# Score products of two attention units in a row in a banded attention and token/channel mixing kernel

## The chip, the cores and the metric

The kernel runs on one core of a Trainium2 chip. The metric is the device time of one execution in microseconds (us); several executions of each kernel are timed, and the median is compared. One more execution is profiled, and all rows of traces below come from it.

## What is computed

A banded softmax attention (batch 2, 8 heads, 768 positions, head size 64) feeds two mixing layers.

```python
# attention: keys kept are the first 8 (n_global) and the last 96 (n_local) up to the query's own
scores = q @ k.T / sqrt(64) - slope[h] * dist        # where kept, else -1e9
a = exp(scores - max(scores)); a = a / (sum(a) + 1e-9)
x = (a @ v) as [2, 768, 512]                          # heads side by side
# token and channel mixing
u = x + (relu(x.T @ w_tok1) @ w_tok2).T
x = u + relu(u @ w_ch1) @ w_ch2
# rotation, second token mixing, last channel layer
theta = x @ w_theta; zr = x * cos(theta); zi = x * sin(theta)
u = x + w_tok_r @ zr + w_tok_i @ zi
out = u + relu(u @ w_ch)
```

The weights arrive as 64-bit words, and the kernel itself turns them into pairs of a high and a low part. A product of mixing layers is three matmuls on such pairs (high by high, high by low, low by high).

## The kernel before

All layers run one after another; the change touches the first, the banded attention, which takes the first 105 us or so. Each engine runs its own instructions strictly in the order in which the program writes them down (a manual schedule), and instructions of different engines wait for each other through semaphores that are put in automatically: a tile that is to be written again waits for the last reader of what was in it, even where that reader stands further down in the program.

**Units.** The attention is cut into 24 units. Unit u covers one batch, one pair of heads (j = 0, 1) and two blocks of 128 queries (ii = 0, 1). Three units make a pair of heads (ip = 0, 1, 2), so there are eight pairs of heads, and each has its own q, k and v from memory. In the first unit of a pair (ip = 0) the first query block sees 128 keys and not 256.

**Stages of a unit.**

- Scores (L434): four products of 64 rows by 256 columns (128 where ip = 0 and ii = 0), two for each head. A head occupies 64 of the 128 rows of TensorE, so the products of the two heads lie in different halves of it. Each product is traced as two matmuls. They write two PSUM tiles `s` (tag `s`, 4 buffers).
- VectorE adds the bias and finds the minimum (L447, four instructions for a unit), ScalarE takes exponentials (four), both in the tiles `e0`, `e1`.
- Turn (L481): up to eight transpositions of 128x128 into two PSUM tiles `t` (2 buffers), copied out to `at0` and `at1`, one copy each, by ScalarE (L493), or, for j = 0 and in passes that start a weight job, by VectorE (L491).
- Values (L403): up to eight products with v, each traced as two matmuls, into the PSUM tile `o` (one buffer). Odd units below 12 write tile `m` instead (one buffer). Then `finish_rows` on VectorE (L387, L391, L396) divides by the sums and frees the PSUM tile, and GpSimd splits the result (L376, L379).

**Passes.** The loop over u makes pass u out of the scores of unit u, the turn of unit u-1 and the values of unit u-2, the transpositions and value products alternating. The last two exponentials of unit u are issued within the turn (`between`). From pass 14 on each pass ends with `fill`: two (later one) parts of the token mixing of the batch that is already through, six matmuls of 512 columns in all (L93, out `mm`), and at the very end the transpositions `columns` (L760, out `ut`).

**Loads.** In a pass with ip = 1 the program writes, after the values, on GpSimd the two memsets of the next pair's v tiles (L357), and on the one DMA queue (SP), in this order: v of the next pair (L364, L366, L367), then q and k of the pair after it (L335, L336). The tiles of v, q and k have two buffers each. The raw weight loads (L122) go through the same queue.

**Weight jobs.** One 128x512 piece of weights is converted in four phases, one phase in each pass: scale (ScalarE, L136 and L137), join (VectorE L142 and L145, then GpSimd L146), high (ScalarE L154), low (VectorE L157). `STARTS` says in which passes a job starts. In a pass without a start the VectorE phases stand right behind the four L447; in a pass with a start they stand within the turn. Seven jobs are for the token mixing; `EARLY` more are pieces of the first channel blocks, of which every block has two. The other channel pieces are converted in the same four phases later: a phase is advanced at every `tick`, three ticks during the token mixing that follows, and then one after every half of `up` (L93, out `gp`) for batch 0. A piece must be through before `up` or `down` of its block reads it.

Of the kernel before, what the change touches and what calls it, by code (L numbers as in the profile page):

```python
# [15 lines left out]
F32 = mybir.dt.float32  # L16
# [9 lines left out]
P = 128  # L26
# [22 lines left out]
WARM_FILL = (4, 2)  # L49
# [12 lines left out]
def r(ap):  # L62
    return ap.bitcast(F32R)
# [17 lines left out]
class Build:  # L81
# [326 lines left out]
    def attention_band(self, pairs_pool, first, h1):  # L408
# [5 lines left out]
        ps_, half = self.ps, len(units) // 2  # L414
        with tc.tile_pool(name="au", bufs=2) as up, tc.tile_pool(name="aa", bufs=2) as ap:

            def scores(u):
                b, hp, ip = units[u]
                t = pairs[(b, hp)]
                n = "_%d" % u  # L420
                mn = up.tile([P, 2, 2], F32, name="mn" + n, tag="mn", bufs=4)
                es = []
                for j in range(2):
                    es.append(up.tile([P, 2, 2 * P], F32, name="e%d" % j + n, tag="e%d" % j))
                ps = [
                    ps_.tile([P, 2, 2 * P], F32, name="s%d" % j + n, tag="s") for j in range(2)
                ]
                kf = t["k"].rearrange("p n w -> p (n w)")
                for ii in range(2):
                    i = 2 * ip + ii  # L430
                    c0 = P if i == 0 else 0
                    for j in range(2):
                        pj = slice(j * D, (j + 1) * D)
                        nc.tensor.matmul(  # L434
                            ps[j][:, ii, c0:],
                            lhsT=t["q"][pj, i * P : (i + 1) * P],
                            rhs=kf[pj, i * KW - P + c0 : i * KW + P],
                            start=True,
                            stop=True,
                        )  # L440
                exps = []
                for ii in range(2):
                    i = 2 * ip + ii
                    c0 = P if i == 0 else 0
                    for j in range(2):
                        e = es[j][:, ii, c0:]
                        nc.vector.tensor_tensor_reduce(  # L447
                            out=e,
                            in0=ps[j][:, ii, c0:],
                            in1=self.base[2 * hp + j][min(i, 1)],  # L450
                            op0=ALU.add,
                            op1=ALU.min,
                            scale=-SCALE,
                            scalar=BIGNUM,
                            accum_out=mn[:, ii, j : j + 1],
                        )
                        exps.append(functools.partial(
                            nc.scalar.activation,
                            out=e,
                            in_=e,  # L460
                            func=AF.Exp,
                            bias=mn[:, ii, j : j + 1],
                            scale=-1.0,
                        ))
                st[u] = dict(e=es)
                return exps

            def turn(u, dve, between):


                b, hp, ip = units[u]
                n = "_%d" % u
                e = st[u]["e"]
                st[u]["at"] = at = []

                def one(j, ii, c):
                    if len(at) == j:
                        at.append(ap.tile([P, 2, 2, P], F32, name="at%d" % j + n, tag="at%d" % j))
                        st[u]["pt"] = ps_.tile([P, 2, 2, P], F32, name="t%d" % j + n, tag="t")
                    pt = st[u]["pt"]  # L480
                    nc.tensor.transpose(  # L481
                        pt[:, ii, c, :], e[j][:, ii, c * P : (c + 1) * P], self.ident
                    )
                    if ii == c == 1:
                        c0 = 1 if ip == 0 else 0
                        pf = pt.rearrange("p a c w -> p (a c) w")[:, c0:, :]
                        af = at[j].rearrange("p a c w -> p (a c) w")[:, c0:, :]
                        if j == 1:
                            between()
                        if j == 0 and dve:  # L490
                            nc.vector.tensor_copy(out=af, in_=pf)  # L491
                        else:
                            nc.scalar.copy(out=af, in_=pf)  # L493

                return [
                    functools.partial(one, j, ii, c)
                    for j in range(2)
                    for ii in range(2)
                    for c in range(2)
                    if ip or ii or c  # L500
                ]
# [32 lines left out]
            N = len(units)  # L534
            fill = collections.defaultdict(list)

            def mix1(b, tb, s, tag):
                return functools.partial(self.token_part, tag, h1, b, tb, s)

            def mix2(s):  # L540
                return functools.partial(self.token_row, "m", h1, 0, s)

            def columns(s):
                return functools.partial(self.turn_row, "t", 0, s)

            for n in range(2 * NS):
                tb, s = divmod(n, NS)
                fill[half + 2 + n // 2].append(mix1(0, tb, s, "m"))
            for s in range(NS):
                fill[N - 4 + s].append(mix2(s))  # L550
            for s in range(4):
                fill[N - 2 + s].append(columns(s))
            for tb in range(NT):
                for s in range(NS - 2):
                    fill[N + 1].append(mix1(1, tb, s, "s"))
            self.load_v(first, 0, 0)
            self.token_jobs()
            pairs[order[1]] = self.load_qk(pairs_pool, *order[1], bufs=2)
            for u in range(N + 2):
                start = u in self.STARTS  # L560
                on_dve, on_act = self.split_tick(start)
                exps = []
                if u < N:
                    b, hp, ip = units[u]
                    oi = u // (NS // 2)
                    exps = scores(u)
                    if u < len(WARM_FILL):
                        self.warm_up(WARM_FILL[u])
                if not start:
                    on_dve()  # L570
                for step in exps[:2]:
                    step()

                def between(late=exps[2:]):
                    for step in late:
                        step()
                    if start:
                        on_dve()
                    on_act()

                turned = 0 <= u - 1 < N
                if not turned:
                    between()
                self.run_steps(
                    turn(u - 1, start and u < N - 4, between) if turned else [],
                    values(u - 2) if 0 <= u - 2 < N else [],
                )
                for step in fill.pop(u, ()):
                    step()
                if u < N and oi + 1 < len(order) and ip == 1:  # L590
                    nx = order[oi + 1]
                    self.tiles_v(pairs_pool, pairs[nx], *nx)
                    self.load_v(pairs[nx], *nx)
                    if oi == 0:
                        self.prefetch(1)
                    if oi + 2 < len(order):
                        pairs[order[oi + 2]] = self.load_qk(pairs_pool, *order[oi + 2], bufs=2)
# [165 lines left out]
    def token_jobs(self):  # L763
# [15 lines left out]

        for i in range(self.EARLY):  # L780
            self.channel_job(*divmod(i, 2))
# [31 lines left out]
    def run(self):  # L813
        nc, tc, dram = self.nc, self.tc, self.dram
        with ExitStack() as es:
# [23 lines left out]

            we = es.enter_context(tc.tile_pool(name="we", bufs=self.EARLY, side="right"))  # L840
            self.early = we
            self.wc = [[None, None] for _ in range(NF)]
            for i in range(self.EARLY):
                self.channel_piece(we, *divmod(i, 2))
# [29 lines left out]
                self.moe(es, a8s, w12p, h1)  # L874

    KW12 = 9
    EARLY = 4
    STARTS = (5, 8, 11, 13, 14, 16, 17, 18, 20, 21, 22)

    def moe_jobs(self, ws, w12p):  # L880

# [6 lines left out]
        for i in range(2 * NF):  # L888
            self.wc_job[divmod(i, 2)] = 0 if i < self.EARLY else self.channel_job(*divmod(i, 2))

# [126 lines left out]
class PhaseB:  # L1017
# [23 lines left out]
    def turn(self, i):  # L1041
        b, s = self.todo[i]
        t = self.xt[i] = self.xtbuf(i)
        x = self.k.x[b][:, s, :]
        self.k.turn_rows("t", x, r(t[:, 0]), r(t[:, 1]), "xt_%d_%dp" % (b, s))
# [239 lines left out]
```

## Time and profile before

| | |
|---|---|
| median of 3 runs | 506.6 us (506.12 to 506.81) |
| the profiled execution, its own time | 506.85 us |
| its span, from the first to the last instruction | 505.1 us |
| TensorE matmul busy | 499.5 us, 99% |
| VectorE, ScalarE, GpSimd busy | 61%, 47%, 32% |

The span is what the trace covers; 1.75 us of the profiled execution's time lie around it. Ends of matmuls are modelled, so rows of TensorE are read by their starts: the distance from one start to the next is what an instruction costs.

### The profile page before, as it was taken

How to read it: one execution, taken by the hardware profiler on the slowest of the kernel's cores; microseconds unless marked ns; L12 is line 12 of the kernel's file. 1: busy time of each engine (PE TensorE's matmuls, PEld its weight loads, DVE VectorE, ACT ScalarE, POOL GpSimd, SP SyncE). 2: the span in 40 equal slices, each digit the busy share in tenths (PEclk: the TensorE clock that was granted, in tenths of full speed). 3: DMA queues.
4: the chain of work that ended last, by engine and by line, in shares of the span. 5: the costliest groups of instructions: out<-in, count | busy, mean ns of one | idle time of the engine just before them, and what ended most of it. 6: DMA issues, size and time to landing. Idle time of an engine off the chain costs nothing.

```text
span 505.1 us, 7724 instructions
## 1 busy us (share of the span) xinstructions
PE 499.5 (99%) x2908; PEld 421.1 (83%) x2908; DVE 309.3 (61%) x671; ACT 235.7 (47%) x458; POOL 163.4 (32%) x175
## 2 busy tenths in 40 slices
PE   9999999999999999999999999999999999999997
PEld 4888878887888888888888888888888889888886
DVE  4688878736877575216473565377888876351342
ACT  6798778714755554113554544435555343222010
POOL 7355444410343333001332151154555533223000
PEclk9999999999999999999999999999999999999999
DMA  6697764202453443002333121222210000000012
GB/s 192 201 262 242 233 212 141 84 3 65 148 150 124 135 126 94 0 1 76 120 120 102 42 78 48 84 84 84 80 46 1 1 1 0 22 21 22 21 64 103
DMA packets 30013, 45.93 MB, mean 91 GB/s; under 512 B 1936, under 2 KB 20880, under 8 KB 29968
## 3 DMA queue, kind: packets, MB, share of 16 engines
q1 hardware_dynamic: 29968, 45.36, 28.8%
q8 instruction: 25, 0.41, 0.3%
q14 instruction: 20, 0.16, 0.1%
HBM read 42.21 MB, written 3.15 MB: 90 GB/s over the span
## 4 chain that ended last, share of the span: by engine, by line
PE 95%; SPq 1%; DMA 1%; ACT 1%; DVE 1%; issue 0%; ACTq 0%
PE gp L93 20%; PE y L93 20%; PE h L93 19%; PE th L93 7%; PE v L93 7%; PE mm L93 6%; PE o L403 6%; PE t L481 4%; PE s L434 4%; DMA k<-k 1%; PE ut L760 1%; SPq L856 0%; DVE xl L710 0%; ACT xh L704 0%; PE xt_1p L760 0%
## 5 line engine op out<-in xcount | busy, mean ns | idle before, releaser
L146 POOL TENSOR_TENSOR cvt<-cvt,cvs 128x512 int32<-128x512 int32 (+1 forms) x57 | 75.8, 1330 | 219.8 <-DVE cvt L145 175.3
L93 PE MATMUL h<-wc,g 128*128 128x512 f32 x432 | 102.1, 390 | 0.0
L93 PE MATMUL gp<-xh,wc 128*128 128x512 f32 (+1 forms) x384 | 99.1, 339 | 0.1
L93 PEld LDWEIGHTS h<-wc,g 128*128 128x128 f32 x432 | 79.6, 188 | 15.4
L706 DVE SCALAR_TENSOR_TENSOR g<-gp,g 128x512 fp32r<-128x512 f32 (+1 forms) x48 | 26.7, 557 | 85.7 <-ACT g L704 85.7
L93 PEld LDWEIGHTS gp<-xh,wc 128*128 128x128 f32 x384 | 67.1, 188 | 9.7 <-DVE xl L710 0.3
L93 PE MATMUL gp<-xl,wc 128*128 128x512 f32 (+1 forms) x192 | 64.9, 338 | 0.0
L704 ACT ACTIVATE g<-gp 128x512 fp32r<-128x512 f32 (+1 forms) x48 | 23.4, 488 | 72.5 <-PE gp L93 72.5
L93 PE MATMUL y<-wri,z 128*128 128x256 f32 (+1 forms) x288 | 52.9, 338 | 0.0
L93 PE MATMUL y<-wri,s 128*128 128x256 f32 (+1 forms) x288 | 52.8, 338 | 0.0
L93 PEld LDWEIGHTS y<-wri,s 128*128 128x128 f32 x288 | 44.8, 188 | 6.8
L93 PEld LDWEIGHTS y<-wri,z 128*128 128x128 f32 x288 | 44.8, 188 | 6.8
L481 PE MATMUL t<-ident,e 128*128 128x128 f32 x176 | 48.1, 285 | 0.3 <-ACT at L493 0.3
L142 DVE SCALAR_TENSOR_TENSOR cvs<-cvt,cvs 128x512 int32<-128x512 int32 (+1 forms) x57 | 44.4, 778 | 0.0
L93 PEld LDWEIGHTS gp<-xl,wc 128*128 128x128 f32 x192 | 36.1, 188 | 5.1
L481 PEld LDWEIGHTS t<-ident,e 128*128 128x128 f32 x176 | 31.7, 184 | 8.1 <-ACT at L493 2.2
L447 DVE CUSTOM_DVE_ANT_0 e<-s,base 128x256 f32<-128x256 f32 (+1 forms) x96 | 32.8, 398 | 9.2 <-PE s L434 8.5
L136 ACT ACTIVATE cvt<-raw 128x512 f32<-128x512 f32 (+1 forms) x57 | 37.3, 655 | 1.9 <-issue 1.9
L137 ACT ACTIVATE cvs<-raw 128x512 int32<-128x512 uint16 (+1 forms) x57 | 37.3, 654 | 0.0
L1075 ACT ACTIVATE w<-w 128x512 f32<-128x512 f32 x12 | 7.6, 633 | 57.3 <-DVE w L1072 57.3
L403 PE MATMUL o<-v,at 128*128 128x65 f32 x192 | 32.3, 252 | 0.0
L403 PEld LDWEIGHTS o<-v,at 128*128 128x128 f32 x192 | 29.8, 196 | 0.0
(136 smaller groups left out, 814.0 us busy)
## 6 DMA issues: line engine op xcount, KB each, us to landing
raw<-w_ch SPq DMA_DIRECT2D x28, 512.0 KB, 3.6
raw<-w_tok SPq DMA_DIRECT2D x21, 512.0 KB, 3.5
k<-k SPq DMA_DIRECT2D x7, 480.0 KB, 5.7
v<-v SPq DMA_DIRECT2D x8, 384.0 KB, 3.7
out<-o SPq DMA_DIRECT2D x11, 256.0 KB, 2.0
q<-q SPq DMA_DIRECT2D x7, 384.0 KB, 5.0
raw<-w_theta SPq DMA_DIRECT2D x4, 512.0 KB, 3.6
a<-v SPq DMA_DIRECT2D x8, 240.0 KB, 4.5
```

What stands on the lines that cost most here:

```text
L93: self.nc.tensor.matmul(out, lhsT=a, rhs=b, start=first and i == 0, stop=last and i == n - 1)
L136: nc.scalar.activation(out=f(t), in_=f(top), func=AF.Copy, scale=2.0**-111)
L137: nc.scalar.activation(out=s, in_=nxt, func=AF.Copy, scale=2.0**-13)
L142: nc.vector.scalar_tensor_tensor(out=s, in0=t, scalar=-(1 << 31), in1=s, op0=ALU.bitwise_and, op1=ALU.bitwise_or)
L146: nc.gpsimd.tensor_tensor(out=t, in0=t, in1=s, op=ALU.add)
L403: self.nc.tensor.matmul(po[:, j * OW : j * OW + D + 1], lhsT=at, rhs=v[:, j * (D + 1) : (j + 1) * (D + 1)], start=first, stop=last,)
L434: nc.tensor.matmul(ps[j][:, ii, c0:], lhsT=t["q"][pj, i * P : (i + 1) * P], rhs=kf[pj, i * KW - P + c0 : i * KW + P], start=True, stop=True,)
L447: nc.vector.tensor_tensor_reduce(out=e, in0=ps[j][:, ii, c0:], in1=self.base[2 * hp + j][min(i, 1)], op0=ALU.add, op1=ALU.min, scale=-SCAL ...
L481: nc.tensor.transpose(pt[:, ii, c, :], e[j][:, ii, c * P : (c + 1) * P], self.ident)
L704: nc.scalar.activation(out=hi, in_=ps, func=AF.Relu if relu else AF.Copy)
L706: nc.vector.scalar_tensor_tensor(out=lo, in0=ps, scalar=0.0, in1=f(hi), op0=ALU.max, op1=ALU.subtract)
L1075: nc.scalar.activation(out=a, in_=t, func=AF.Abs)
```

## The change

The score products of two units are issued one behind the other: units 0 and 1 (with the warm-up matmuls between them), unit 2 alone, then 3 and 4, 5 and 6, and so on to 21 and 22, and 23 alone, each pair in the odd pass. The turn and the values move one pass back (turn of u-2 and values of u-3 in pass u), so the loop has one pass more and `fill` moves by one. The exponentials wait in a list `late`, from which four are issued at the start of an odd pass and two at each of two places later on. The tiles `e0` and `e1` get four buffers instead of two. `EARLY` goes from 4 to 2, so two pieces (channel block 1) are no longer converted during the attention but first in the mixing, and `STARTS` has 9 passes instead of 11.

```diff
--- before.py
+++ after.py
@@ -421,7 +421,9 @@
                 mn = up.tile([P, 2, 2], F32, name="mn" + n, tag="mn", bufs=4)
                 es = []
                 for j in range(2):
-                    es.append(up.tile([P, 2, 2 * P], F32, name="e%d" % j + n, tag="e%d" % j))
+                    es.append(
+                        up.tile([P, 2, 2 * P], F32, name="e%d" % j + n, tag="e%d" % j, bufs=4)
+                    )
                 ps = [
                     ps_.tile([P, 2, 2 * P], F32, name="s%d" % j + n, tag="s") for j in range(2)
                 ]
@@ -465,7 +467,7 @@
                 st[u] = dict(e=es)
                 return exps
 
-            def turn(u, dve, between):
+            def turn(u, dve, first, second):
 
 
                 b, hp, ip = units[u]
@@ -485,8 +487,7 @@
                         c0 = 1 if ip == 0 else 0
                         pf = pt.rearrange("p a c w -> p (a c) w")[:, c0:, :]
                         af = at[j].rearrange("p a c w -> p (a c) w")[:, c0:, :]
-                        if j == 1:
-                            between()
+                        (first, second)[j]()
                         if j == 0 and dve:
                             nc.vector.tensor_copy(out=af, in_=pf)
                         else:
@@ -545,45 +546,59 @@
 
             for n in range(2 * NS):
                 tb, s = divmod(n, NS)
-                fill[half + 2 + n // 2].append(mix1(0, tb, s, "m"))
+                fill[half + 3 + n // 2].append(mix1(0, tb, s, "m"))
             for s in range(NS):
-                fill[N - 4 + s].append(mix2(s))
+                fill[N - 3 + s].append(mix2(s))
             for s in range(4):
-                fill[N - 2 + s].append(columns(s))
+                fill[N - 1 + s].append(columns(s))
             for tb in range(NT):
                 for s in range(NS - 2):
-                    fill[N + 1].append(mix1(1, tb, s, "s"))
+                    fill[N + 2].append(mix1(1, tb, s, "s"))
             self.load_v(first, 0, 0)
             self.token_jobs()
             pairs[order[1]] = self.load_qk(pairs_pool, *order[1], bufs=2)
-            for u in range(N + 2):
+
+
+            late = []
+
+            def emit(n):
+                for _ in range(min(n, len(late))):
+                    late.pop(0)()
+
+            for u in range(N + 3):
                 start = u in self.STARTS
                 on_dve, on_act = self.split_tick(start)
-                exps = []
+                new = {0: (0, 1), 1: (), 2: (2,)}.get(u, (u, u + 1) if u % 2 else ())
+                for n in new:
+                    if n < N:
+                        late += scores(n)
+                        if n < len(WARM_FILL):
+                            self.warm_up(WARM_FILL[n])
+                if new:
+                    emit(4)
                 if u < N:
                     b, hp, ip = units[u]
                     oi = u // (NS // 2)
-                    exps = scores(u)
-                    if u < len(WARM_FILL):
-                        self.warm_up(WARM_FILL[u])
                 if not start:
                     on_dve()
-                for step in exps[:2]:
-                    step()
-
-                def between(late=exps[2:]):
-                    for step in late:
-                        step()
+
+                def first():
+                    if not new:
+                        emit(2)
+
+                def second():
+                    emit(2)
                     if start:
                         on_dve()
                     on_act()
 
-                turned = 0 <= u - 1 < N
+                turned = 0 <= u - 2 < N
                 if not turned:
-                    between()
+                    first()
+                    second()
                 self.run_steps(
-                    turn(u - 1, start and u < N - 4, between) if turned else [],
-                    values(u - 2) if 0 <= u - 2 < N else [],
+                    turn(u - 2, start and u < N - 3, first, second) if turned else [],
+                    values(u - 3) if 0 <= u - 3 < N else [],
                 )
                 for step in fill.pop(u, ()):
                     step()
@@ -874,8 +889,8 @@
                 self.moe(es, a8s, w12p, h1)
 
     KW12 = 9
-    EARLY = 4
-    STARTS = (5, 8, 11, 13, 14, 16, 17, 18, 20, 21, 22)
+    EARLY = 2
+    STARTS = (6, 9, 12, 14, 15, 17, 18, 20, 22)
 
     def moe_jobs(self, ws, w12p):
```

## Rows read from the trace of the kernel before

**Rows 1.** The page, busy time of the engines, share of the span, instructions.

```profile
PE 499.5 (99%) x2908; PEld 421.1 (83%) x2908; DVE 309.3 (61%) x671; ACT 235.7 (47%) x458; POOL 163.4 (32%) x175
```

**Rows 2.** Timeline of TensorE around unit 7: start, length, line, instructions merged.

```profile
26.80 0.34 PE L403 MATMUL o<-v,at 128*128 128x65 f32 x2
...
28.13 0.33 PE L481 MATMUL t<-ident,e 128*128 128x128 f32 x1
28.29 0.33 PE L403 MATMUL o<-a,at 128*128 128x65 f32 x2
28.46 0.28 PE L481 MATMUL t<-ident,e 128*128 128x128 f32 x1
28.58 0.34 PE L403 MATMUL o<-v,at 128*128 128x65 f32 x2
```

**Rows 3.** The same unit's score matmuls, from three narrow windows of that timeline.

```profile
27.07 0.70 PE L434 MATMUL s<-k,q 64*128 64x256 f32 x3
...
27.39 0.59 PE L434 MATMUL s<-k,q 64*128 64x256 f32 x3
...
27.81 0.38 PE L434 MATMUL s<-k,q 64*128 64x256 f32 x2
```

**Rows 4.** Timeline of TensorE, scores of units 3, 4, 6 and two first transpositions.

```profile
11.36 0.33 PE L481 MATMUL t<-ident,e 128*128 128x128 f32 x1
...
13.95 0.93 PE L434 MATMUL s<-k,q 64*128 64x128 f32 x8 [0.44 <-DMA k<-k]
14.81 0.33 PE L481 MATMUL t<-ident,e 128*128 128x128 f32 x1
...
17.24 1.14 PE L434 MATMUL s<-k,q 64*128 64x256 f32 x8
...
23.77 0.93 PE L434 MATMUL s<-k,q 64*128 64x128 f32 x8
```

**Rows 5.** Timeline of the DMA queue: keys of the third pair, v of the fifth, keys of the sixth.

```profile
15.82 1.62 SPq L336 DMA_DIRECT2D k<-k  x1
...
42.57 0.38 SPq L364 DMA_DIRECT2D v<-v  x1
...
45.17 0.42 SPq L336 DMA_DIRECT2D k<-k  x1
```

**Rows 6.** Tile k, windows around the issues at 15.82 and at 45.17.

```profile
DMA to landing us min/median/max: 7.1/7.1/7.1
...
DMA to landing us min/median/max: 5.5/5.5/5.5
```

**Rows 7.** The page, costliest groups: the reduction of the scores.

```profile
L447 DVE CUSTOM_DVE_ANT_0 e<-s,base 128x256 f32<-128x256 f32 (+1 forms) x96 | 32.8, 398 | 9.2 <-PE s L434 8.5
```

**Rows 8.** Timeline of TensorE: first matmul of a fill, next scores.

```profile
62.61 0.48 PE L93 MATMUL mm<-xh,w 128*128 128x512 f32 x1
...
64.19 0.49 PE L434 MATMUL s<-k,q 64*128 64x256 f32 x2
```

**Rows 9.** Timeline of VectorE: a join, a finish, the next unit's first reduction.

```profile
57.25 0.55 DVE L142 SCALAR_TENSOR_TENSOR cvs<-cvt,cvs 128x384 int32<-128x384 int32 x1
57.83 0.36 DVE L145 TENSOR_SCALAR cvt<-cvt 128x384 int32<-128x384 int32 x1
...
62.84 0.16 DVE L387 TENSOR_SCALAR rc<-o 128x4 f32<-128x4 f32 x1
...
63.25 0.42 DVE L396 TENSOR_TENSOR x<-o,rc 128x256 f32<-128x256 f32 x1
...
65.55 0.41 DVE L447 CUSTOM_DVE_ANT_0 e<-s,base 128x256 f32<-128x256 f32 x1
```

**Rows 10.** Timeline of all engines, where block 1 of `up` begins.

```profile
131.11 0.68 DVE L157 SCALAR_TENSOR_TENSOR wc<-cvt,wc 128x512 fp32r<-128x512 f32 x1
...
131.29 0.47 PE L93 MATMUL gp<-xh,wc 128*128 128x512 f32 x1
```

**Rows 11.** Timeline of TensorE, pass 24, the only wait late in the attention.

```profile
98.31 0.33 PE L481 MATMUL t<-ident,e 128*128 128x128 f32 x1 [0.34 <-ACT at L493]
```

## The prediction

> **What bounds the kernel now.** I read the page first: TensorE is busy 99% of the span [rows 1]. Since the ends of its matmuls are modelled, I then went to its timeline and read starts only. Around unit 7 one transposition follows another at 0.29 us with a value product in between, with no hole [rows 2]. So in the attention the order of TensorE's own instructions sets the time, and what counts is what an instruction costs there, what makes TensorE wait, and what is queued behind the instruction that waits.
>
> The same timeline shows what a separate group of scores costs beyond its columns. Within unit 7 four steps lie between the starts 27.07, 27.39, 27.81 and the first transposition at 28.13 [rows 2, 3]. The middle two together take 0.42, so a pair of products (one for each head) streams in about 0.215. The first and the last step take 0.32 each: 0.105 too much, twice. The group starts 0.26 after the last value product (26.80 to 27.06), where a transposition starts 0.17 after one (28.29 to 28.46): 0.09 more. The first transposition is followed after 0.16 and not 0.12: 0.04 or 0.05 more. In sum a separate group costs 0.35 us that a group joined to the one before does not pay.
>
> **The change, part by part.**
>
> Joined groups. There were 24 groups and there will be 14 (units 0 and 1 still have warm-up matmuls between them, 2 and 23 stand alone, ten pairs are joined). Ten times 0.35 is **-3.5 us**. It all lies on TensorE's path.
>
> The keys of the second pair of heads. Unit 3 needs them, and already waits 0.44 for them, until 13.95 [rows 4]. Their load is issued at the start and doesn't move. But the turn and the values now stand one pass later: before unit 3's scores TensorE used to have the turn of unit 1 and the values of unit 0, which began at 11.36 and took until about 13.35. In the new order they stand behind the scores of units 3 and 4, in the queue of the engine that waits. So TensorE comes to unit 3 some 2.0 us earlier, finds no keys, and waits 2.4 instead of 0.4: **+2.0 us**.
>
> The keys of the third pair. They are issued at 15.82 and land 7.1 later, at 22.9 [rows 5, 6]; unit 6 took them at 23.77 without a wait [rows 4]. Now TensorE has, from 13.95: the scores of 3 and 4, 0.86 (13.95 to 14.81, unit 3) and four pairs at 0.215, 0.86, together 1.7; a pass of turn and values without unit 0's missing parts is 17.24 - 14.81 = 2.43 less 0.14 of switching, 2.3, and the one with unit 0 is 2.0; then the scores of unit 5, 0.09 + 0.97. It stands before unit 6 at about 21.0, and waits until 23.0: **+2.0 us**.
>
> Both together, checked another way: at the scores of unit 6 the old order had done everything up to the turn of 4 and the values of 3. The new one begins unit 6 at 23.0, 0.7 earlier, with two passes of turn and values outstanding. From 17.24 to 23.77 lie two score groups at 1.07 and these two passes, so they are 6.53 - 2.14 - 2 x 0.14 = 4.1. It is 3.4 behind, and eight joined groups are still to come, -2.8: **+0.6** in all. This much I hold for nearly certain, since the loads' times don't hang on the change.
>
> The keys of the fifth pair. Their load stands behind v of the fourth pair in the queue, and that tile is free only after the values of unit 5, now in pass 8 and no longer in pass 7. From 23.05 by the same prices: unit 6's scores 0.86, two passes 4.1, scores of 7 and 8 2.0, two passes 4.5: the values of 5 end at about 34.6. From the issue of v to that of the next keys are 2.6 (42.57 to 45.17) and to their landing 5.5 to 7.1 more [rows 5, 6]: 42.7 to 44.3. TensorE reaches unit 12, now in pass 11, after scores 1.8, two passes 4.3 and unit 11's scores 1.1: 41.8. The wait is between 0.9 and 2.5 if nothing else delays TensorE; the waits below come before it and shorten it, down to 0.3. I take **+1.0**. Later pairs have the six fill matmuls in each pass as cover, and I put them at nothing; without the fill each would cost as much.
>
> VectorE behind eight reductions. One reduction takes 32.8 / 96 = 0.34 [rows 7]; two units in a row make eight, 2.75 us, while the eight pairs take TensorE 1.7. No score tile is late, since the four buffers are free again a pass before. What is late is what stands behind them on VectorE: `finish_rows`, which frees the only buffer `o` for the values of the next pass. From unit 12 on every unit uses it. Before, a fill and a score group, about 2.6 us, lay between the last value product and the next pass's first. In the passes after an odd one only the fill is left: 62.61 to 64.19, 1.5 us [rows 8]. Take pass 21 from its start. The first reduction starts at 1.36 as it did at 65.55 after 64.19 (a conversion of the token mixing stands ahead) [rows 8, 9]. Two of the eight are half as long, so they end at 3.9; the low phase of one job, 0.68 at most [rows 10], and the join of another, 57.25 to 58.19, 0.94, follow, and `finish_rows` takes 62.84 to 63.67, 0.83 [rows 9]: 6.3. TensorE is through its scores at 1.7, its turn and values at 3.7, its fill at 5.2, and wants `o` at 5.35: it waits 1.0. In pass 19 there is only a join, in pass 17 a copy and a low phase, and the same sum gives about 0.2 each; in pass 15 the short unit 12 ends early and gives none. That is **+1.4**; nothing at the low end, and 3 at the high one if the join is slow each time.
>
> At this place a rule of the Trainium skill speaks against the change. "TensorEngine Tiling (Array Packing)", section "PSUM Bottleneck", says that tiling speeds up TensorE but not the evacuation of PSUM, and that the evacuation may become the bottleneck. The rows agree that VectorE takes longer for eight reductions than TensorE for the eight pairs; by the rule alone TensorE would wait at every joined group (rival D).
>
> Pass 9 has the same shape without fill: a job starts there, so the copy of unit 7's first tile is on VectorE behind the eight reductions. At the price of the nearest row of its shape, 0.68 [rows 10], it ends some 0.4 after the values of pass 10 want it: **+0.4**, between 0 and 0.9.
>
> The two pieces that move to the mixing. Each takes VectorE 0.94 + 0.68 [rows 9, 10], off TensorE's path there as in the attention. But the first is then the one that block 1 of `up` reads. The piece in its place ended its low phase at 131.79, and block 1 began at 131.29 and would want the low part with its third matmul, about 0.5 later [rows 10]: **+0.2**, 0 to 0.5.
>
> The four buffers for exponentials cost nothing; they only allow the rest, since with two the reductions of unit u+1 would have to wait for transpositions of the pass after. The end: the one late wait of before, 0.34 in pass 24 [rows 11], may go, but two passes without scores stand there now instead of one. I take 0, -0.3 to +0.7.
>
> The sum: 0.6 + 1.0 + 1.4 + 0.4 + 0.2 = +3.6 on the profiled execution's 506.85, so 510.45. That execution is 0.25 above the median of 506.6; against the median I forecast **510.2 us**.
>
> **The rivals.**
>
> A: only the two waits at the start are real. TensorE's place in the later passes hangs on rows that I add up over 20 us, and a gap of 0.5 us anywhere hides the rest. Then +0.6: 507.2. For it: before, VectorE had over 1 us to spare at `o`. Against it: three places would all have to be off.
>
> B, on the other side: faster. The keys are there in time, because the loads land sooner when TensorE's order changes. It decides at the second pair before 11.6 and the third before 21.0. Then -3.5, or with the later waits but the fifth pair's about -1.5: 503.1 to 505.1. Against it: the old trace shows TensorE waiting for these keys, and no instruction ahead of their loads moves.
>
> D: VectorE holds TensorE at every joined group. Eight reductions less eight pairs is 1.0 us, ten times: 506.6 + 0.6 + 10, about 517. Against it: over two passes, some 6.5 us, VectorE has 2.75 for reductions and 1.7 for finishes, and catches up.
>
> **How the numbers follow.** A measurement of this kernel can tell about 0.2%, 1 us, from no change. My forecast has 74 in 100, A 16, B 7, D 3. A lies within 0.2%, B is faster, the rest slower: 0.07, 0.16, 0.77. The forecast's own range: all later waits at their low ends give +0.6 to +0.9, at their high ends 0.6 + 2.5 + 3 + 0.9 + 0.5, but the fifth pair's wait shrinks by what comes before it, so about +6.2. The range leaves out B, D and the lower part of A: 507.0 to 512.8.
>
> **What the profile would show.** Right: score groups of 16 matmuls with no step of 0.32 in the middle; waits for `k` of about 2.4 at unit 3, 2 at unit 6 and near 1 at unit 12; transpositions or value products that start late in passes 10, 18, 20 and 22, with VectorE named; the attention longer by 3 to 4 us and the mixing as before but for its first blocks. Wrong: no wait at unit 6, so the loads landed sooner (B); no waits past unit 12 (A); steps of 0.32 within joined groups, so nothing was saved; a wait in every even pass (D).

## The result, and the profile after

| | before | after |
|---|---|---|
| median | 506.71 us (506.12 to 507.65) | 512.97 us (512.3 to 516.9) |
| the profiled execution, its own time | 506.85 us | 513.18 us |
| its span | 505.1 us | 511.4 us |
| mean granted clock of TensorE | 1.000 | 0.993 |

Four runs each. The ratio over all runs is 1.0138, 95% interval [1.0112, 1.0164]; the medians alone give 1.0124, since one run of after took 516.9. By the medians the kernel is slower by 6.3 us, where 3.6 were predicted; 512.97 is just above the range's end of 512.8. The spans differ by the same 6.3. The page gives TensorE as much busy time as before [rows 1], in a longer span, and the row of the granted clock, which had no dent before, has one in its second slice (a slice is 12.8 us).

```profile
PE 499.8 (98%) x2908; PEld 424.4 (83%) x2908; DVE 311.4 (61%) x671; ACT 236.8 (46%) x458; POOL 163.8 (32%) x175
...
PEclk9799999999999999999999999999999999999999
```

The list of TensorE's waits of after: line, what it waited for, us in total, times, longest.

```profile
PE s L436 <- DMA k<-k: 5.3, 3, 2.7
...
PE o L403 <- DVE x L396: 0.9, 1, 0.9
```

So the keys come first, three times, and VectorE makes TensorE wait at `o` once and not at every joined group. (In the new kernel the scores stand in L436, the turn in L483, the copies in L492 and L494, the reduction in L449.) The same waits in place, from the timeline of TensorE after; the brackets hold the idle time before a row and what ended it.

```profile
10.39 0.88 PE L483 MATMUL t<-ident,e 128*128 128x128 f32 x6
...
13.98 3.36 PE L436 MATMUL s<-k,q 64*128 64x128 f32 x16 [2.72 <-DMA k<-k]
17.27 0.47 PE L483 MATMUL t<-ident,e 128*128 128x128 f32 x1
...
17.86 0.42 PE L483 MATMUL t<-ident,e 128*128 128x128 f32 x1
...
22.86 1.79 PE L436 MATMUL s<-k,q 64*128 64x256 f32 x16
24.58 0.33 PE L483 MATMUL t<-ident,e 128*128 128x128 f32 x1
...
28.85 2.00 PE L436 MATMUL s<-k,q 64*128 64x256 f32 x16
30.78 0.33 PE L483 MATMUL t<-ident,e 128*128 128x128 f32 x1
...
39.75 0.33 PE L483 MATMUL t<-ident,e 128*128 128x128 f32 x1 [0.43 <-DVE at L492]
...
44.51 0.93 PE L436 MATMUL s<-k,q 64*128 64x128 f32 x8 [1.19 <-DMA k<-k]
...
57.71 1.57 PE L436 MATMUL s<-k,q 64*128 64x128 f32 x14 [1.37 <-DMA k<-k]
...
91.33 0.41 PE L403 MATMUL o<-a,at 128*128 128x65 f32 x2 [0.95 <-DVE x L396]
...
101.89 0.33 PE L483 MATMUL t<-ident,e 128*128 128x128 f32 x1 [0.19 <-DVE xl L725]
...
106.14 0.33 PE L483 MATMUL t<-ident,e 128*128 128x128 f32 x1 [0.28 <-DVE xl L725]
```

Unit 3 gets its keys at 13.98, as before at 13.95 [rows 4], but TensorE now stands idle for 2.72 us ahead of them. Units 7 and 8 take 28.85 to 30.78, 1.93 for both. Narrow windows of the same timeline show the middle, where unit 7 ends and unit 8 begins at 29.82, and unit 6 behind unit 5:

```profile
29.60 0.60 PE L436 MATMUL s<-k,q 64*128 64x256 f32 x4
...
29.82 0.60 PE L436 MATMUL s<-k,q 64*128 64x256 f32 x4
```

```profile
23.83 0.39 PE L436 MATMUL s<-k,q 64*128 64x128 f32 x4
```

The step in the middle is 0.22, not the 0.32 that a separate group has at each end [rows 3]. Units 12 and 15 wait for keys too. What the prediction has nothing of is between 13.98 and 22.86: the scores of units 3 and 4 take 3.29 (to 17.27), where those of units 5 and 6, with as many products, take 1.72 (to 24.58). The windows of after over this stretch say why: from, to, length, busy time and instructions of TensorE, its loads, VectorE, ScalarE and GpSimd, then the granted clock, the DMA share and GB/s.

```profile
12.00:14.00 2.00, 0.02 (x2) 0.05 (x2) 0.00 (x0) 1.40 (x4) 1.28 (x3) 0.78 0.09 34
14.00:16.00 2.00, 2.00 (x12) 1.82 (x14) 0.26 (x3) 0.00 (x0) 0.00 (x0) 0.50 0.70 209
16.00:18.00 2.00, 2.00 (x12) 1.29 (x9) 1.49 (x11) 1.49 (x4) 0.00 (x0) 0.50 1.12 250
18.00:20.00 2.00, 2.00 (x14) 2.00 (x13) 0.91 (x6) 0.62 (x2) 0.00 (x0) 0.51 1.04 388
20.00:22.00 2.00, 2.00 (x22) 2.00 (x22) 0.77 (x3) 2.00 (x6) 0.54 (x2) 1.00 0.59 230
```

In the wait of 2.72 us the granted clock falls to 0.50, the level of 1.2 GHz, and it stays there for three windows; TensorE does 12 to 14 instructions in each instead of 22. So the late keys brought 2.3 us of new idle time and then some 6 us at half rate, in which TensorE does about 3 us less work than at full rate.

Why unit 15 waits shows in the DMA queue's timeline after,

```profile
36.54 0.37 SPq L364 DMA_DIRECT2D v<-v  x1
...
38.55 0.43 SPq L336 DMA_DIRECT2D k<-k  x1
...
47.95 0.38 SPq L364 DMA_DIRECT2D v<-v  x1
...
51.10 0.43 SPq L336 DMA_DIRECT2D k<-k  x1
```

and in the landing time of tile `k` behind the issue at 51.10:

```profile
DMA to landing us min/median/max: 6.5/6.5/6.5
```

51.10 and 6.5 are 57.6, and unit 15 begins at 57.71. The keys of unit 15 stand behind v, whose tile is free only after the values of unit 8, which stand behind unit 12's wait. In the kernel before these keys were there long before TensorE came: issued at 45.17 and landed 5.5 later, at 50.7 [rows 5, 6], for scores that begin at 54.60 (timeline of TensorE before):

```profile
54.60 0.93 PE L434 MATMUL s<-k,q 64*128 64x128 f32 x8
```

Last, VectorE's timeline after in pass 21, behind which TensorE waits at `o`:

```profile
86.35 0.28 DVE L449 CUSTOM_DVE_ANT_0 e<-s,base 128x128 f32<-128x128 f32 x1
...
88.48 0.42 DVE L449 CUSTOM_DVE_ANT_0 e<-s,base 128x256 f32<-128x256 f32 x1
...
88.83 0.56 DVE L157 SCALAR_TENSOR_TENSOR w<-cvt,w 128x384 fp32r<-128x384 f32 x1
89.30 0.69 DVE L142 SCALAR_TENSOR_TENSOR cvs<-cvt,cvs 128x512 int32<-128x512 int32 x1
...
90.36 0.15 DVE L387 TENSOR_SCALAR rc<-o 128x4 f32<-128x4 f32 x1
...
90.77 0.42 DVE L396 TENSOR_TENSOR x<-o,rc 128x256 f32<-128x256 f32 x1
```

Eight reductions (86.35 to 88.83), a low phase, a join and only then the finish (90.36) that frees `o`: the predicted chain, in the predicted order.

### The profile page after: what moved, and what is told of

The parts are those of the page before. It is cut to its first block, busy times and chain, and to the rows that moved or that the text cites. A ratio compares the mean times of both kernels' runs of the same rounds, so it can differ in the third digit from the quotient of the medians.

```text
span 511.4 us, 7689 instructions
## 1 busy us (share of the span) xinstructions
PE 499.8 (98%) x2908; PEld 424.4 (83%) x2908; DVE 311.4 (61%) x671; ACT 236.8 (46%) x458; POOL 163.8 (32%) x175
## 4 chain that ended last, share of the span: by engine, by line
PE 91%; DMA 4%; DVE 2%; SPq 2%; issue 1%; ACT 0%; POOL 0%; ACTq 0%
PE gp L93 20%; PE y L93 20%; PE h L93 19%; PE th L93 7%; PE v L93 7%; PE mm L93 6%; PE o L403 5%; DMA k<-k 4%; PE t L483 3%; PE s L436 3%; PE ut L775 1%; DVE xl L725 1%; DVE e L449 0%; SPq L871 0%; ACT xh L719 0%
## 5 line engine op out<-in xcount | busy, mean ns | idle before, releaser
L483 PE MATMUL t<-ident,e 128*128 128x128 f32 x176 | 48.2, 287 | 0.9 <-DVE xl L725 0.5
L566 ACT ACTIVATE e<-e,mn 128x256 f32<-128x256 f32 (+1 forms) x96 | 39.9, 482 | 14.5 <-DVE mn L449 14.5
L449 DVE CUSTOM_DVE_ANT_0 e<-s,base 128x256 f32<-128x256 f32 (+1 forms) x96 | 32.2, 398 | 10.4 <-PE s L436 9.0
L483 PEld LDWEIGHTS t<-ident,e 128*128 128x128 f32 x176 | 32.3, 188 | 5.9 <-issue 1.7
```

The lines of the kernel that those rows point to most:

```text
L449: nc.vector.tensor_tensor_reduce(out=e, in0=ps[j][:, ii, c0:], in1=self.base[2 * hp + j][min(i, 1)], op0=ALU.add, op1=ALU.min, scale=-SCAL ...
L483: nc.tensor.transpose(pt[:, ii, c, :], e[j][:, ii, c * P : (c + 1) * P], self.ident)
L566: late.pop(0)()
```

## The experiments

Two theories. Theory 1: the pass that the turn and the values lag behind makes TensorE reach the keys too early, and the wait lowers its clock. Theory 2: the eight reductions in a row on VectorE hold TensorE at the joined groups. Each diff is against the changed kernel, except where another is named. Every ratio is to the kernel before, timed again beside each run.

**The joined groups without the added lag** (`e1_joined_short`).

```diff
-            for u in range(N + 3):
+            for u in range(N + 2):
...
-                    turn(u - 2, start and u < N - 3, first, second) if turned else [],
-                    values(u - 3) if 0 <= u - 3 < N else [],
+                    turn(u - 1, start and u < N - 4, first, second) if turned else [],
+                    values(u - 2) if 0 <= u - 2 < N else [],
...
-    STARTS = (6, 9, 12, 14, 15, 17, 18, 20, 22)
+    STARTS = (5, 8, 11, 13, 14, 16, 17, 19, 21)
```

(The fill moves back by one pass as well.)

> The joined score groups stay (10 of them), but turn and values stand as in the kernel before: turn of unit u-1 and values of unit u-2 in pass u. Theory 1 (the pass that turn and values lost brought TensorE to the keys too early, and the clock fell in the wait): at unit 3 the wait is 0.4 again and the granted clock stays 1.0; at unit 6 a wait of about 1.8 is left, at unit 12 0.5 to 1; 506.7 - 3.5 + 1.8 + 0.8 + 1.0 (the buffer o behind eight reductions), about 506.8 us, between 505.5 and 508. Theory 2 (eight reductions in a row on VectorE are what costs): near the changed kernel, 511 us or more.

Measured: 509.86 us, 1.0064 [1.0042, 1.0087]. The wait at unit 3 is gone: its scores begin at 13.98 straight behind the work before them. But unit 6, joined to unit 5, waits 2.23 (1.8 expected), and the clock falls behind it. TensorE's timeline of this kernel, then its windows:

```profile
23.71 1.15 PE L436 MATMUL s<-k,q 64*128 64x128 f32 x8 [2.23 <-DMA k<-k]
```

```profile
24.00:26.00 2.00, 2.00 (x15) 1.44 (x13) 1.03 (x7) 0.69 (x3) 0.00 (x0) 0.57 1.04 298
```

About half of the loss is gone, so the lag is a cause. The time is still 3 us over my 506.8: joining alone puts unit 6 one pass of turn and values earlier, which I had priced as a wait, but not the fall of the clock behind it. The six runs lie by their mean granted clock: 508.19 and 508.85 at 1.000, 509.76 and 509.96 at 0.997, 511.04 and 511.71 at 0.993. So runs of one kernel differ by some 3 us together with their clock; a clock 0.7% lower over 508 us is worth 3.6, enough for it. Only one of the six has a trace, so that nothing else differs between them is not shown. The two runs at full clock are still some 2 us slower than the kernel before.

**The lag without joined groups** (`e4_lag_alone`).

```diff
-                new = {0: (0, 1), 1: (), 2: (2,)}.get(u, (u, u + 1) if u % 2 else ())
+                new = (u,) if u < N else ()
```

> The changed kernel with one unit's scores in each pass, not two: nothing is joined, but turn and values stand one pass later. Theory 1: the wait for the keys of unit 3 is about 2.4 us and the clock falls behind it, so 2 us and some 3 us of slow clock are lost, and no 3.5 us are won: 510 to 512 us. Theory 2 (eight reductions): 506.7 to 507.5 us.

Measured: 510.38 us, 1.0071 [1.0055, 1.0088], as theory 1 expects. The wait is longer than the 2.4 expected: in this execution TensorE starts its last transpositions ahead of unit 3 at 9.51, in that of the changed kernel at 10.39. TensorE's only wait of over half a microsecond after the warm-up is the one at unit 3, 3.68 us (timeline of this kernel), and the clock falls behind it (windows):

```profile
14.06 0.72 PE L436 MATMUL s<-k,q 64*128 64x128 f32 x6 [3.68 <-DMA k<-k]
```

```profile
14.00:16.00 2.00, 1.94 (x13) 1.41 (x14) 0.71 (x5) 0.37 (x2) 0.00 (x0) 0.66 0.69 206
16.00:18.00 2.00, 2.00 (x13) 2.00 (x13) 0.49 (x4) 1.71 (x5) 0.00 (x0) 0.50 1.18 238
```

No group is joined here, VectorE never has eight reductions in a row, and still 3.7 us are lost. Theory 2 has no part in this loss.

**The clock kept up over the wait** (`e2_warm_wait`): matmuls on zeros fill the idle time ahead of unit 3.

```diff
+                if u == 3:
+                    self.warm_up(14)
                 for n in new:
```

> The changed kernel with 14 matmuls on zeros (512 columns, 0.216 us each) ahead of the scores of unit 3, which fill the wait for its keys. Theory 1: the granted clock stays 1.0 from 14 to 20 us, the score group of units 3 and 4 takes 1.7 us and not 3.3; but TensorE then comes to unit 6 before its keys, so a wait of nearly 2 us comes there and only about 1 to 2 us of the 513 are won, more if the later loads move forward too. Rival: the clock's fall costs all of the 3 us by which the slow stretch is longer, 510 us.

Measured: 512.15 us, 1.0116 [1.0087, 1.0144]. That is 0.8 under the kernel after, and the two intervals overlap, so the gain itself is not shown; the rival's 510, the whole 3 us, lies outside the interval. The timeline of TensorE, and one of its windows:

```profile
13.92 1.79 PE L436 MATMUL s<-k,q 64*128 64x128 f32 x16
...
23.14 0.93 PE L436 MATMUL s<-k,q 64*128 64x128 f32 x8 [1.93 <-DMA k<-k]
```

```profile
14.00:16.00 2.00, 2.00 (x20) 1.67 (x21) 1.05 (x7) 0.71 (x3) 0.00 (x0) 1.00 0.81 220
```

This is the start as predicted: full clock, unit 6 at 23.14 (23.0 predicted) after a wait of 1.93 (2.0). In the changed kernel unit 6's scores begin at 23.83, behind those of unit 5. So between these two executions the fall of the clock costs 0.7 there, not the whole 3 us, because full speed only brings TensorE to the next late keys. How late these are differs: they land 7.3 behind their issue here and 6.3 in the trace of the changed kernel, at 22.2, where full speed could have won up to 1.7.

**All keys there from the start** (`e3_after_firstkeys`, and the same edit to the kernel before, `e8_before_firstkeys`).

```diff
                 b, hp, ip = units[u]
-                t = pairs[(b, hp)]
+                t = pairs[(0, 0)]
```

> The changed kernel, but all scores are made from q and k of the first pair of heads (the other loads are still issued and go unread), so no score waits for a load. Theory 1: no wait and no slow clock at unit 3, none at 6, 12 and 15; what is left is -3.5 for the joined groups, +1.0 at the buffer o, +0.6 in pass 10, +0.5 at the end: about 505.3 us, faster than before. Theory 2: 510 us or more.

> The kernel before with all scores from q and k of the first pair (the other loads issued and unread). Control for the same edit of the changed kernel, which came to 505.15: here only the wait of 0.44 at unit 3 can go, so 506.2 us; anything lower by more than 1 us would mean that the edit itself wins time (fewer distinct operands, loads that nobody waits for).

(These two kernels leave out the queries and keys of seven of the eight pairs: every score is made from those of the first pair. The other loads are still issued, and nobody reads them.)

Measured: 505.15 us, 0.9968 [0.9958, 0.9979], for after so edited, and 505.89 us, 0.9983 [0.9974, 0.9993], for before. The late keys with the clock behind them are therefore 512.97 - 505.15 = 7.8 us in the changed kernel and 506.71 - 505.89 = 0.8 in the old, of which 0.44 is the one wait in its trace: they cost the change 7.0. Everything else in it wins 0.7; the two intervals just overlap, so that this small gain is barely told from none. What waits TensorE keeps in the edited kernel after (list of its waits within the attention):

```profile
PE o L403 <- DVE x L396: 0.9, 1, 0.9
PE t L483 <- DVE xl L725: 0.5, 2, 0.3
PE t L483 <- DVE at L492: 0.4, 1, 0.4
PE o L403 <- ACT at L494: 0.2, 1, 0.2
```

These are 2.0 us, against 3.5 for the joins; the kernel before with the same edit keeps 0.6. Theory 2 is true in its place (pass 22) and small.

**The moved pieces alone** (`e9_before_early2`, diff against the kernel before).

```diff
-    EARLY = 4
-    STARTS = (5, 8, 11, 13, 14, 16, 17, 18, 20, 21, 22)
+    EARLY = 2
+    STARTS = (5, 8, 11, 13, 14, 16, 17, 19, 21)
```

> The kernel before with EARLY = 2 and nine starts (5, 8, 11, 13, 14, 16, 17, 19, 21): only the two moved pieces of channel block 1. All theories: 506.7 us, plus 0 to 0.5 where block 1 of the channel mixing waits for its low part. A gain of 1 us or more would mean that conversions held the attention up before.

Measured: 506.58 us, 0.9995 [0.9986, 1.0004]. Nothing that can be told from no change.

**Joined in even passes** (`e5_even_short`, diff against the first experiment), so that the three units of a pair of heads meet their keys elsewhere in a group.

```diff
-                new = {0: (0, 1), 1: (), 2: (2,)}.get(u, (u, u + 1) if u % 2 else ())
+                new = {0: (0,), 1: (1,), 2: (2,), 3: (3,)}.get(u, () if u % 2 else (u, u + 1))
```

> As the run with joined groups and turn and values at their old distance, but the joined pairs are 4 and 5, 6 and 7, to 22 and 23, so that the first unit of the third pair of heads (6) leads its group. Theory 1: no wait of 2 us at unit 6, so no fall of the clock; waits of about 0.3 at unit 9 and 0.8 at unit 15, which now end a group; 1 to 1.5 us behind VectorE; 506.7 - 3.5 + 0.3 + 0.8 + 1.4, about 505.7 us (504.5 to 507). Theory 2 (eight reductions in a row): 509 us or more.

Measured: 510.0 us, 1.006 [1.0046, 1.0074]: a miss. Unit 6 no longer waits, but unit 3 does for 1.37 and unit 15 for 2.8, and the clock falls behind the latter (windows of this kernel):

```profile
54.00:56.00 2.00, 1.28 (x12) 0.98 (x13) 0.35 (x3) 0.17 (x2) 0.00 (x0) 1.00 0.89 281
56.00:58.00 2.00, 2.00 (x15) 2.00 (x15) 1.54 (x7) 1.56 (x4) 0.00 (x0) 0.58 1.20 222
```

Unit 15 now ends the group of pass 14 and so stands ahead of the first fill, as in the changed kernel. Up to unit 3 TensorE has the order of the first experiment, which had no wait there; the keys landed 6.6 us behind their issue here and 5.3 there, so this wait seems to belong to the execution and not to the edit. The profiled run, 512.29, is the slowest of five; the two at full clock took 508.95 and 509.41.

**q and k ahead of v in the queue** (`e6_after_keysahead`), in all pairs but the first; the same edit on the kernel in even passes is `e7_even_short_keysahead`.

```diff
+                    if oi > 0 and oi + 2 < len(order):
+                        pairs[order[oi + 2]] = self.load_qk(pairs_pool, *order[oi + 2], bufs=2)
                     self.tiles_v(pairs_pool, pairs[nx], *nx)
                     self.load_v(pairs[nx], *nx)
                     if oi == 0:
                         self.prefetch(1)
-                    if oi + 2 < len(order):
                         pairs[order[oi + 2]] = self.load_qk(pairs_pool, *order[oi + 2], bufs=2)
```

> The changed kernel with q and k of the pair after next written ahead of v of the next pair in the DMA queue, from the third load on. If the keys of the fifth and sixth pair are late because their issue stands behind a v tile that the values free a pass later, the waits at unit 12 (1.24 in the changed kernel's trace) and unit 15 (1.44) go, and the start stays as it is: 513.0 - 2.7, about 510.3 us. Rival (the DMA engines are simply full there): the waits stay, 512.5 to 513.5 us.

Measured: 510.6 us, 1.0104 [1.0063, 1.0145]. The waits of units 12 and 15 are gone, those of units 3 and 6 stay (2.08 and 1.24 in the profiled run, with the clock at 0.50 and 0.77 between 14 and 18 us). By the medians the two later waits are worth 2.4, near their 1.19 and 1.37. The intervals of the two kernels overlap, so the size is not shown by the times; that the waits come from v standing ahead of k in the queue is shown by the trace, from which they are gone.

> Both edits together: pairs from 4 and 5 on, old distance, keys ahead of v. Theory 1: the waits at units 9 and 15 shrink too: about 505 us, faster than the kernel before by 1 to 2 us. Rival: v is late in its place, 506 us or more.

Measured: 507.04 us, 0.9998 [0.9985, 1.0011]: equal to the kernel before, 2 us over what I expected and in the rival's range, but TensorE has no wait for v. The clock is full and the keys are nearly in time, so by its price the 3.5 of the joins should be won; the list of TensorE's waits within its attention shows the waits that stand against them:

```profile
PE o L403 <- DVE x L396: 1.3, 2, 0.9
PE t L483 <- ACT cvt L136: 0.6, 1, 0.6
PE s L436 <- DMA k<-k: 0.6, 1, 0.6
PE t L483 <- ACT at L494: 0.4, 1, 0.4
```

**The weight jobs started in other passes**, to take VectorE's job phases from behind the eight reductions. Three kernels change `STARTS`: the changed kernel with all keys at hand (`e3_after_firstkeys`) with (6, 9, 11, 13, 15, 17, 19, 21, 23) (`e10_firstkeys_oddjobs`); the kernel in even passes with the keys ahead of v (`e7_even_short_keysahead`) with (5, 8, 10, 12, 14, 16, 18, 20, 22) (`e11_even_evenjobs`); and the same with this:

```diff
                 if new:
-                    emit(4)
+                    emit(2 * len(new) if u < 4 else 4)
...
-    STARTS = (5, 8, 11, 13, 14, 16, 17, 19, 21)
+    STARTS = (5, 7, 9, 11, 13, 16, 18, 20, 22)
```

(`e12_version`).

> The changed kernel with all scores from the first pair's q and k (505.15 us), and its job starts moved to odd passes (6, 9, 11, 13, 15, 17, 19, 21, 23), so that from pass 15 on the joins and low phases stand in the passes with no scores. If finish_rows behind eight reductions and a job's phases is what TensorE waits for at the buffer o (1.04 in pass 22), that wait goes: 504.1 us, between 503.8 and 504.6. Rival (the eight reductions alone hold it, whatever the jobs do): 505 us, the wait stays.

> The run with pairs from 4 and 5 on, old distance, keys ahead of v (507.04 us), with job starts in even passes (5, 8, 10, 12, 14, 16, 18, 20, 22): there the even passes have the scores, so joins and low phases fall into passes without. The wait of 1.04 at the buffer o in pass 21 goes, and the 0.8 in pass 9 or 10 may move: about 505.8 us, faster than the kernel before by about 1 us. Rival: the waits come back in other passes, 506.5 to 507.5 us.

> The run with pairs from 4 and 5 on, old distance, keys ahead of v (507.04 us), with job starts at 5, 7, 9, 11, 13 (odd, where a pass has no scores and no fill follows) and 16, 18, 20, 22 (even, so that joins and low phases fall into passes without scores once the buffer o is alone), and with two exponentials, not four, ahead of the turn in passes 0 to 3. From the trace of that run: the waits of 1.04 at the buffer o, 0.77 in pass 9 and 0.42 in pass 2 go: about 505 us, faster than the kernel before by 1 to 2 us. Rival: as in the run before, waits of the same size come back behind ScalarE, 506.5 us or more.

Measured: 506.46 us, 0.9994 [0.9985, 1.0003]; 506.95 us, 1.0009 [0.9998, 1.0019]; 507.83 us, 1.0031 [1.0019, 1.0042]. The first is 1.3 over the kernel it was made from, where it should have been 1 under it. Its list of waits, within the attention:

```profile
PE t L483 <- DVE at L492: 0.8, 3, 0.4
PE t L483 <- ACT at L494: 0.8, 2, 0.4
PE o L403 <- ACT at L494: 0.5, 1, 0.5
```

The wait at `o` for VectorE is gone, so the job's phases, and not the eight reductions alone, made it. The jobs now stand in the passes where the copies of the turn are due, and these are late instead; all listed waits are 2.4 us for 2.0, which does not place the whole 1.3. The other two only move such waits about: both lie in their rivals' ranges, and in the last five waits for ScalarE's copies are 2.2 us and two for keys 1.6. I found no version with the whole computation that beats the kernel before.

## Why the prediction was right in sign and too small

The main step that failed is "Later pairs ... I put them at nothing", with the fill as cover; the second is the start, where the clock's fall has no term. By its own steps:

- **Joined groups, -3.5: the mechanism is right.** Two units take 1.93 (28.85 to 30.78), no step of 0.32 in between. With all keys at hand the change wins 0.7 net. That is -3.5, 1.4 more of waits behind VectorE and ScalarE than the old kernel so edited has (2.0 and 0.6), and another 1.4 that I can't place, so the full 3.5 are priced from steps and not measured as a whole.
- **Keys of the second pair, +2.0: right.** 2.72 idle against a predicted 2.4; what came behind it, the clock, is in the next step.
- **Keys of the third pair, +2.0 (both and the joins together +0.6): this step failed**, by what it left out. It priced the scores and the passes behind unit 3's wait at full clock; the trace has 0.50 for some 6 us, so TensorE came to unit 6 after the keys (landed at 22.2) and there was no wait. The working was right where the clock stays up: the warmed kernel starts unit 6 at 23.14. With the clock's fall it is 23.83, so the step is +1.4 rather than +0.6. "Nearly certain, since the loads' times don't hang on the change" was too sure as well: in eight profiled runs these keys landed 6.3 to 8.1 us behind their issue, and the run with keys ahead of v has both, the fallen clock and a wait of 1.24 at unit 6.
- **Keys of the fifth pair, +1.0: right,** 1.19 idle, by the named chain (v's tile, then v, then k in one queue). TensorE came there at 43.3 for 41.8, and the keys landed at 44.4, at the late end of 42.7 to 44.3; that the size fits is partly luck.
- **Later pairs at nothing, with the fill as cover: this step failed,** and cost the most: 1.37 idle at unit 15. The diff moves `fill` by one pass too: before, the first six matmuls stood at the end of pass 14, ahead of unit 15; now they stand at the end of pass 15, behind it. They take about 1.5, so they would have covered the 1.37; that is worked out, no run moves the fill alone. In the old kernel they hid nothing: the keys were there 3.9 us before unit 15. What used that up is the load, which landed at 57.6 for 50.7 since the start, the lag and unit 12's wait had delayed the values that free v's tile. The keys-ahead run takes both waits away, with 2.4 us by the medians.
- **VectorE behind eight reductions, +1.4:** pass 22 is right (0.95 idle, 1.0 predicted), the 0.2 in each of passes 18 and 20 didn't come. The rule of the Trainium skill in "TensorEngine Tiling (Array Packing)", section "PSUM Bottleneck", that evacuation may become the bottleneck (it says so of a fourfold speedup), holds for this one pass. As the main cause it is refuted by the run with all keys at hand, which has VectorE's eight reductions ten times and is faster than before.
- **Pass 9's copy, +0.4:** 0.43 idle. **Moved pieces, +0.2:** nothing, in the trace and by themselves. **The end, 0:** about +0.3; two waits for VectorE's last work stand there (101.89 and 106.14), 0.36 and 0.44 late by their starts, instead of the one of before, which was 0.51 late [rows 11].

Summed by starts: 1.4 for the start with all the joins, 1.24 and 1.44 at units 12 and 15, 1.04 in pass 22, 0.58 behind the copy of pass 10, 0.3 at the end: 6.0 of the 6.3. The forecast had 0.6, 1.0, 0, 1.4, 0.4, 0 and 0.2 for the moved pieces, 3.6 in all: most of the miss is unit 15's 1.44 and the start's 0.8. Of the rivals, A (only the start) and D (every joined group) fell; B, the keys in time, was wrong at units 3, 12 and 15. Not settled is why the joins with all keys in time (`e7`) come out even: the waits are listed, but the two tries on it moved them and did not remove them.

## What to carry to other kernels

When work is reordered to save switching, ask for every wait on a load that stays in the program what stood ahead of it as cover, and whether that cover moved with the edit; the fill that would have covered unit 15's wait here was moved behind it by the same diff. A wait of TensorE has to be priced with the clock that it finds afterwards, and a delay only up to the next load that is late anyway. Try the reordering, and the old order, with one early load read throughout: these two runs told here that the saving was 0.7 us net and the late loads cost 7.

## What the runs showed of the hardware

The fall of the clock was not expected. In the profiled runs the granted clock went from 1.00 to between 0.50 and 0.66 in the windows behind waits of 2.08, 2.23, 2.72, 2.8 and 3.68 us, and stayed at 1.00 behind 1.93 and 1.37. In the changed kernel the windows put it at about 13.1 to 19.9 us: a transposition with its value product took 0.53 (17.86 to 18.39) and 0.29 once it was back. The same kernel doesn't always meet it alike: the six runs of the first experiment have mean clocks of 1.000, 0.997 and 0.993, two each, and the four of the changed kernel 0.997, 0.997, 0.993 and 0.989, at 512.30, 512.77, 513.18 and 516.90 us. The Trainium skill, "TensorE: Matmul & The Clock Gate", section "What's actually happening", says that the throttled clock is the default state and that activity releases it; the rows agree, 0.50 behind the idle time and 1.00 after TensorE had worked on, and the warmed kernel, busy through the wait, stayed at 1.00 in its profiled run.

The landing of a load is no constant either. In eight profiled runs the keys of the second pair landed 5.2 to 6.6 us behind an issue at about 8.1, and those of the third 6.3 to 8.1 behind one at about 15.8; by that alone a wait for them can be a microsecond or more longer or shorter in another execution.
